# Recurrent-memory attention and feed-forward kernel: merged transposes, token sums earlier, flushed fill work, outputs in row order, and a regrouped preparation of the feed-forward part

## The chip, the cores and the metric

The kernel runs on one core of one Trainium2 chip. The metric is device microseconds of one execution, the median of several. The core has five engines that run their own instruction streams and wait for each other by semaphores: TensorE (PE; its weight loads are listed as PEld), VectorE (DVE), ScalarE (ACT), GpSimd (POOL) and SyncE (SP, which here only issues DMAs). PE adds up in PSUM buffers, from which ACT and DVE copy ("evacuate") results to SBUF.

## The reference

B = 1, S = 2048 tokens, D = 640, 32 heads of 128, 8 memory rows, segments of 32 tokens, F = 1728; bfloat16 in and out.

```python
mem = mem0
for s in range(S // 32):                       # 64 segments, one after another
    h = concat([mem, layernorm(x)[s*32:(s+1)*32]])      # 8 + 32 rows
    q, k, v = h @ Wq, h @ Wk, h @ Wv                    # per head
    p = softmax(where(mask, q k^T / sqrt(128), -1e9))   # the 8 memory rows see all 40 keys,
                                                        # a token the keys up to its own
    o = (p v) @ Wo
    mem = o[:8]                                # feeds the next segment
    outs.append(o[8:])
h = x + concat(outs)
out = h + relu(layernorm(h) @ w1 + b1)**2 @ w2 + b2
```

## The kernel before, in words

The 64 segments form NB = 16 blocks of four steps (sp = 0 to 3); each step is one segment, and the memory rows that leave a step enter the next one through mem_to_hT (L283), so the steps are a serial chain. A step works on 32 rows in its main path: 8 memory rows and the first HD = 24 tokens. The last TL = 8 tokens of the four segments of a block are taken together as a "tail" of 32 rows, since nothing in the chain needs them at once. The tail's q, k and v passes of block b + 1 are cut into units (tail_pass_fill, L241: ten units of four matmuls for each of q, k and v, and for q and k two "late" units that transpose the row), the tail's output projection of block b - 1 into eight units (wo_tail_fill, L268). These units wait in the list `fill`, and run_fill(n) (L236) runs n of them at places in a step where the chain would leave PE without work: three (F1) after the memory softmax's sums, four (F2) before the output projection, two after it and one behind mem_to_hT.

main_step (L341) goes through a step in this order: two q passes of 20 matmuls each (half, L206 for the matmuls; evacuation in L199 on ACT or L201 on DVE); the token values of the step before (token_values, L307); the first k pass, a transpose of the first half of q (turn, L219: four 128x128 transposes, then one 512-wide evacuation), the second k pass, the second half of q, the first half of k; twelve matmuls of the first v pass, the second half of k, eight more; twelve of the second v pass; scores (L385, L389); the exponentials on ACT (L392 for the memory columns, L398 for tokens, L400 for the tail); two masks on Pool (L402, L403); the memory softmax's sums pz (L408), its reciprocal rz and diagonal rd on DVE, the values po (L425), the spread reciprocal pb (L429), rs on ACT (L432), oT on DVE (L436); then the output projection wo_pass (L226), 128 matmuls with the function sums (L444) in its middle: four one-row sums pzk (L448, L450), their reciprocal rk on DVE (L453), a spread copy rb on Pool (L454). Behind the projection two transposes pr (L461) turn rb over, and DVE writes the normalized token weights pnk and pnl (L463, L464), which token_values uses in the next step.

The order on PE, ACT, DVE and Pool is the order of the code down to order.close() (L513); after it a scheduler sets it. PSUM has two "mm" buffers (all passes, output projections, and fill units from their first to their last), two "pt" buffers (transposes and small sums) and four for values. Each step's o goes to DRAM by one DMA (o_main, L304), each block's tail by one (o_tail, L279).

The start loads wq, wk, wv in chunks of 128 rows on SP; their fifth chunk is packed into the partitions by four DMAs of 32 rows each on ACT's queue (L171), and wo is split between SP and ACT.

The feed-forward part (FFN) goes through four tiles t of NT = 512 tokens. prep(t) (L538) loads for each of its four blocks of 128 rows x and eight pieces of o_main and o_tail, adds them (L549), takes the layernorm's statistics (L118, L121) on DVE, its root by fourteen small Pool operations (L122 to L129), applies it (L139), transposes on PE (L554), evacuates on ACT (L556), and adds b2 on Pool (L558). Then come 14 groups of five matmuls (L567) with relu on ACT (L570) and the square on DVE (L571), prep(t + 1), and 8 groups of 14 matmuls (L582) with the last add (L584) and the output's DMA. The FFN's weights take the place of wq in the last step.

## Time and profile before

| what | value |
|---|---|
| median of 5 runs | 1388.39 us (1386.1 to 1396.4) |
| the profiled execution's own time | 1388.16 us |
| its span | 1386.5 us |
| PE / DVE / ACT / POOL busy | 88% / 36% / 34% / 18% of the span |
| first main q pass of block 1, of block 15, start of the last step | 128.83, 1118.80, 1167.30 us |
| first FFN matmul | 1220.83 us |

The span runs from the first to the last instruction in the trace; 1.66 us of the profiled execution lie around it. A row of the timeline has the start, the duration, engine, line, operation, `out<-in` by the program's tile names (`ps` and `pw` PSUM of a pass and of an output projection, `pt` of transposes, `hT` and `hTt` the transposed inputs of main path and tail), how many instructions were put together, and in brackets the idle time ahead and what ended it. Matmuls overlap in the pipeline, so a group's cost is best read from its start to the next group's start.

### The profile page before, as it was taken

To read this page: it belongs to the slowest core of one execution; us is meant where nothing else is said; L and a number is where in the kernel's file an instruction comes from. 1 tells how busy PE (TensorE), PEld (TensorE's weight loads), DVE (VectorE), ACT (ScalarE), POOL (GpSimd) and SP (SyncE) were. 2 spreads that over 40 slices of the span, in tenths; PEclk is the share of its full clock that TensorE was granted. 3 is DMA by queue.
4 is the path that set the end of the run, shared out by engine and by line. 5 is a ranking of instruction groups with operands and counts; after the bars stand their busy time and mean duration, and the time that the engine had idled before them with its cause. 6 is when DMAs were issued, how large, how long until landed. Compare 5 with 4: busy or idle time off the path is not lost.

```text
span 1386.5 us, 69365 instructions
## 1 busy us (share of the span) xinstructions
PE 1215.0 (88%) x32248; PEld 704.4 (51%) x32248; DVE 503.5 (36%) x1400; ACT 465.4 (34%) x1001; POOL 256.4 (18%) x813
## 2 busy tenths in 40 slices
PE   0699999899999999989998999999999998378879
PEld 0255555555555555555555555555555555334444
DVE  1033434343334343433333334343434334234332
ACT  0233333333333333333333343333333333033212
POOL 4011111111111111111111112121212111334340
PEclk9899999999999999999999999999999999679999
DMA  9900000000000000000000000000000002402200
GB/s 230 378 27 6 12 6 12 6 13 6 12 6 12 6 12 6 12 6 12 6 12 4 12 6 12 6 12 6 8 6 8 6 7 80 121 19 58 55 23 20
DMA packets 37762, 43.92 MB, mean 32 GB/s; under 512 B 22816, under 2 KB 34880, under 8 KB 35552
## 3 DMA queue, kind: packets, MB, share of 16 engines
q1 hardware_dynamic: 34400, 33.46, 8.1%
q10 hardware_dynamic: 2656, 5.77, 1.5%
q8 instruction: 252, 4.13, 1.2%
q0 software_dynamic: 416, 0.26, 0.1%
q14 instruction: 38, 0.31, 0.1%
HBM read 33.44 MB, written 5.94 MB: 28 GB/s over the span
## 4 chain that ended last, share of the span: by engine, by line
PE 75%; DVE 6%; DMA 5%; ACT 5%; issue 4%; POOL 3%; SPq 1%; ACTq 0%; POOLq 0%; DVEq 0%
PE ps L206 39%; PE pw L226 11%; PE pt L219 6%; PE psy L582 4%; PE ps L226 3%; ACT row L199 2%; DMA wq<-in_A_Wq_dram 2%; PE psf L567 2%; PE po L425 2%; DVE row L201 2%; PE pss L389 1%; DMA wk<-in_A_Wk_dram 1%; PE po L312 1%; PE pss L385 1%; PE po L318 1%
## 5 line engine op out<-in xcount | busy, mean ns | idle before, releaser
L206 PEld LDWEIGHTS <-hT 128*32 128x32 bf16 x7680 | 179.4, 96 | 203.2 <-issue 45.3
L199 ACT CAST row<-ps 128x512 bf16<-128x512 f32 x192 | 112.7, 587 | 329.7 <-PE ps L206 313.8
L206 PE MATMUL ps<-wv,hT 128*32 128x512 bf16 x2560 | 177.8, 383 | 15.5 <-DVE vr L201 12.0
L226 PE MATMUL pw<-wo,oT 128*32 128x160 bf16 x8320 | 174.0, 235 | 17.2 <-issue 9.4
L201 DVE CAST row<-ps 128x512 bf16<-128x512 f32 x128 | 88.5, 691 | 232.4 <-PE ps L206 232.4
L206 PE MATMUL ps<-wk,hT 128*32 128x512 bf16 x2560 | 161.6, 381 | 8.5 <-ACT row L199 5.3
L226 PEld LDWEIGHTS <-oT 128*32 128x32 bf16 x8320 | 148.6, 98 | 37.5 <-issue 17.3
L206 PE MATMUL ps<-wq,hT 128*32 128x512 bf16 x2560 | 153.0, 381 | 14.2 <-ACT row L199 11.0
L219 PEld LDWEIGHTS <-row 128*128 128x128 bf16 x1280 | 76.0, 98 | 105.7 <-issue 98.6
L402 POOL TENSOR_TENSOR pk_s<-pk_s,mask_m 128x192 bf16<-128x192 bf16 x64 | 45.7, 714 | 439.6 <-ACT pk_s L398 439.5
L219 PE MATMUL pt<-ident,row 128*128 128x128 bf16 x1280 | 113.6, 222 | 14.2 <-DVE rz L416 9.8
L324 POOL COPY oTt<-oT 128x256 bf16<-128x256 bf16 x64 | 25.6, 400 | 315.8 <-DVE oT L201 310.5
L201 DVE CAST vr<-ps 128x512 bf16<-128x512 f32 x64 | 44.3, 692 | 109.2 <-PE ps L206 109.2
L199 ACT COPY kT<-pt 128x512 bf16<-128x512 bf16 x128 | 75.3, 589 | 17.6 <-PE pt L219 17.5
L582 PE MATMUL psy<-fw,fk 128*128 128x320 bf16 x448 | 73.1, 313 | 0.0
L199 ACT CAST oT<-po 128x256 bf16<-128x256 f32 x128 | 41.5, 375 | 93.2 <-PE po L318 93.2
L567 PE MATMUL psf<-fk,fw 128*128 128x512 bf16 (+1 forms) x280 | 63.8, 387 | 5.8 <-ACT fv L570 3.5
L206 PEld LDWEIGHTS <-hTt 128*32 128x32 bf16 x1920 | 40.3, 97 | 55.8 <-issue 24.4
L199 ACT COPY qT<-pt 128x512 bf16<-128x512 bf16 x64 | 37.4, 585 | 88.5 <-PE pt L219 88.5
L454 POOL CAST rb<-rk 128x256 bf16<-128x256 f32 x64 | 26.4, 412 | 193.8 <-DVE rk L453 193.8
L436 DVE TENSOR_TENSOR oT<-po,rs 128x128 bf16<-128x128 f32 x128 | 31.3, 286 | 74.2 <-ACT rs L432 74.2
L206 PE MATMUL ps<-wq,hTt 128*32 128x512 bf16 x640 | 48.2, 397 | 10.9 <-DMA wq<-in_A_Wq_dram 6.7
(108 smaller groups left out, 1480.7 us busy)
## 6 DMA issues: line engine op xcount, KB each, us to landing
wq<-in_A_Wq_dram SPq DMA_DIRECT2D x4, 1024.0 KB
wk<-in_A_Wk_dram SPq DMA_DIRECT2D x4, 1024.0 KB
wv<-in_A_Wv_dram SPq DMA_DIRECT2D x4, 1024.0 KB
o_main<-o SPq DMA_DIRECT2D x65, 40.0 KB
xt<-in_A_x_dram SPq DMA_DIRECT2D x16, 160.0 KB
wo<-in_A_Wo_dram ACTq DMA_DIRECT2D x2, 1280.0 KB
wo<-in_A_Wo_dram SPq DMA_DIRECT2D x2, 1280.0 KB
fv<-in_A_x_dram SPq DMA_DIRECT2D x16, 160.0 KB
```

Of the source, the lines that this page charges most:

```text
L199: nc.scalar.copy(out=out_, in_=in_)
L201: nc.vector.tensor_copy(out=out_, in_=in_)
L206: nc.tensor.matmul(ps[32 * g:32 * g + 32, :], lhsT=lhs(c), rhs=w[:, c, g * EG + n * 512:g * EG + (n + 1) * 512], start=(c == 0), stop=(c = ...
L219: nc.tensor.transpose(out=pt[:, k * 128:(k + 1) * 128], in_=row[:, i * 128:(i + 1) * 128], identity=ident[:])
L226: nc.tensor.matmul(ps[32 * g:32 * g + 32, 0:DG], lhsT=lhs(h), rhs=wo[:, h, g * DG:(g + 1) * DG], start=(h == 0), stop=(h == H - 1))
L324: nc.gpsimd.tensor_copy(out=oTt[:, :, sp * TL:(sp + 1) * TL], in_=oT[:, :, SEG:NQ])
L402: nc.gpsimd.tensor_tensor(out=pkh, in0=pkh, in1=mask_m[:], op=ALU.mult)
L425: nc.tensor.matmul(po[:, i * SEG:(i + 1) * SEG], lhsT=v[:, i * E:(i + 1) * E], rhs=pbd[:, a, i].rearrange("p g q -> p (g q)"), start=(a == ...
L436: nc.vector.tensor_tensor(out=oT[:, k * 16:(k + 1) * 16, 0:M].rearrange("p (g i) q -> p g i q", g=2), in0=pov[:, gs], in1=rs[:].rearrange( ...
L454: nc.gpsimd.tensor_copy(out=rb[:], in_=rk[:].unsqueeze(2).to_broadcast([128, 2 * G, SEG]))
L567: nc.tensor.matmul(ps[0:fs, :], lhsT=w1[:, c, fc * 128:fc * 128 + fs], rhs=hnT[:, c, :], start=(c == 0), stop=(c == DC - 1))
L582: nc.tensor.matmul(ps[:, 0:320], lhsT=f1T[0:fs, fc, k * 128:(k + 1) * 128], rhs=w2[0:fs, fc, cs], start=(fc == 0), stop=(fc == FC - 1))
```

## The change

- turn() transposes all eight chunks of a row in one visit and evacuates 1024 columns at once: q's on ACT, k's on DVE. Both turns stand behind the first v pass, which is now in one piece.
- The token sums come from a matmul with a block matrix of ones (onesblk), which gives them already spread: two matmuls right behind pb. The reciprocal is taken on 256 columns; rb, the two pr matmuls and sums() are gone, the output projection is in one piece, and pnk and pnl stand behind mem_to_hT.
- run_fill counts microseconds written into the code (0.22 for a pass unit, 0.29 for an output unit, 0.6 for a late turn) instead of units: 0.8, 0.9 and 0.4 at three places, and everything that is left at the step's end. The late turns come one step later.
- o is written in row order to one DRAM tensor a_rows: four DMAs a step of 24x160 and sixteen a block of 8x160 instead of one each. The FFN loads one 128x640 piece of it a block.
- The fifth weight chunks go DRAM to DRAM (w4s) by twelve DMAs on ACT's queue, and come back as one 128-partition load each on SP. All of wo is loaded on SP.
- prep is split: prep_loads, prep_rows (adds, statistics, one root for four blocks, applies, b2 adds) and prep_turn (transposes). prep_rows(0) stands ahead of the last token_values; in the FFN loop loads and rows for t + 1 stand ahead of the fc loop and the transposes behind it. The FFN's weights and the first rows are loaded in the last step; the output leaves in halves.

On ACT, a step before, from the evacuation of k's row: one evacuation for q's second half, two for k, the exponentials (`p`, `pk_s`, `p_lz`), and then evacuations of fill units among the rest.

```order
L199 CAST row<-ps 128x512
L199 COPY qT<-pt 128x16x32
L199 COPY kT<-pt 128x512 x2
L392 ACTIVATE p<-pss 128x8x2x8
L199 CAST vr<-ps 128x512
L398 ACTIVATE pk_s<-pss 128x256
L400 ACTIVATE p_lz<-pss 128x8x8
L199 CAST row<-ps 128x512
L199 COPY kTt<-pt 128x512
L432 COPY rs<-pb 128x256
```

The same stretch of ACT's stream now:

```order
L208 CAST row<-ps 128x512
L208 COPY qT<-pt 128x32x32
L439 ACTIVATE p<-pss 128x8x2x8
L208 CAST vr<-ps 128x512
L448 ACTIVATE pk_s<-pss 128x256
L450 ACTIVATE p_lt<-pss 128x64
L482 COPY rs<-pb 128x256
```

q's evacuation has become one for the whole row, k's have gone to DVE, and the evacuations of the fill units come after rs.

On PE, before, the token sums in the middle of the output projection (`pw` is the projection, LDWEIGHTS loads the operand that stays in the array; the brackets name the engines whose semaphores are waited for).

```order
L226 MATMUL pw<-wo,oT 32x160
L448 LDWEIGHTS pk_s [waits Pool_49]
L448 MATMUL pzk<-ones_76,pk_s 128x4 [waits Activation_49]
L450 LDWEIGHTS p_lz [waits Pool_49]
L450 MATMUL pzk<-ones_76,p_lz 128x4
L448 LDWEIGHTS pk_s
L448 MATMUL pzk<-ones_76,pk_s 128x4
L450 LDWEIGHTS p_lz
L450 MATMUL pzk<-ones_76,p_lz 128x4
L226 LDWEIGHTS oT [waits DVE_49]
L226 MATMUL pw<-wo,oT 32x160
```

On PE now, behind the spread reciprocal pb of the memory rows:

```order
L475 MATMUL po<-pbd,vt 128x32
L479 LDWEIGHTS ones_109
L479 MATMUL pb<-rd,ones_109 128x256 [waits DVE_49]
L484 LDWEIGHTS onesblk [waits PE_49,Activation_49]
L484 MATMUL pzk<-pk_s,onesblk 128x256 [waits Pool_49]
L485 LDWEIGHTS onesblk
L485 MATMUL pzk<-p_lt,onesblk 128x8x8 [waits Pool_49]
L215 LDWEIGHTS hTt
L215 MATMUL ps<-wv,hTt 32x512
```

The sums and their two waits for Pool's masks stand ahead of the second fill and of the whole output projection instead of in its middle.

On DVE, before, the end of attention (`pnk` and `pnl` are the last step's token weights, `oT` the last token values, `o` the last output) and the first block of prep(0):

```order
L463 TENSOR_TENSOR pnk<-pk_s,pr 128x256
L464 TENSOR_TENSOR pnl<-p_lz,pr 128x64
L201 CAST oT<-po_36946 128x8x32
L201 CAST oT<-po_36948 128x8x32
L231 CAST o<-pw 128x160
L549 TENSOR_TENSOR fv<-fv 128x640
L118 BN_STATS lnst<-fv 128x6 x2
L121 BN_AGGR lnmv<-lnst 128x2
L139 TENSOR_SCALAR fv<-fv,lnmv,lnrs 128x640
```

The same place on DVE now (from the last of four adds with statistics that stand behind pnl):

```order
L383 TENSOR_TENSOR fv<-fv 128x640
L115 BN_STATS lnst<-fv 128x6 x2
L386 BN_AGGR fmv<-lnst 128x2
L132 TENSOR_SCALAR fv<-fv,fmv,lnrs 128x640 x4
L210 CAST oT<-po_36725 128x8x32
L210 CAST oT<-po_36727 128x8x32
L383 TENSOR_TENSOR fv<-fv 128x640
L115 BN_STATS lnst<-fv 128x6 x2
```

The four adds, statistics and applies of prep_rows(0) have come ahead of the copies of the last token values, and the adds of t = 1 follow at once.

The core of the diff:

```diff
-        def turn(row, j, dst, eng):
+        def turn(row, dst, eng):
             pt = psum_t.tile([128, 1024], BF16, tag="pt", name="pt")
-            for k in range(4):
-                i = j * 4 + k
+            for i in range(HG):
...
-            evac(eng, dst, pt[:, 0:512].rearrange("p (i g r) -> p i g r", i=4, g=G))
+            evac(eng, dst, pt[:].rearrange("p (i g r) -> p i g r", i=HG, g=G))
...
-        def run_fill(n, eng="act"):
-            while n > 0 and fill:
-                fill.pop(0)(eng)
-                n -= 1
+        def run_fill(us, eng="act"):
+            while us > 0.1 and fill:
+                f, t = fill.pop(0)
+                f(eng)
+                us -= t
...
             half(wk, lhs, 0, kr, "act")
-            turn(qr, 0, qT[:, 0:4, :, 0:SEG], "dve")
             half(wk, lhs, 1, kr, "dve")
-            turn(qr, 1, qT[:, 4:8, :, 0:SEG], "act")
-            turn(kr, 0, kT[:, 0:4], "act")
...
+            half(wv, lhs, 0, vr, "dve")
+            turn(qr, qT[:, :, :, 0:SEG], "act")
+            turn(kr, kT[:], "dve")
...
+            pzk = psum_t.tile([128, 512], F32, tag="pt", name="pzk")
+            nc.tensor.matmul(pzk[:, 0:NK], lhsT=onesblk[:], rhs=pk_s[:], start=True, stop=False, skip_group_check=True)
+            nc.tensor.matmul(pzk[:, 0:NK].rearrange("p (i q) -> p i q", q=SEG)[:, :, HD:SEG], lhsT=onesblk[:],
+                             rhs=p_lt[:], start=False, stop=True, skip_group_check=True)
...
-            run_fill(F2)
...
-            o = wo_pass(b * 4 + sp, sums)
...
+            rk = s1.tile([128, NK], F32, tag="rs", name="rk")
+            nc.vector.reciprocal(out=rk[:], in_=pzk[:, 0:NK])
+            run_fill(0.9)
...
+            o = wo_pass(b * 4 + sp)
+            run_fill(0.4)
...
-            run_fill(1)
+            nc.vector.tensor_tensor(out=pnk[:], in0=pk_s[:], in1=rk[:], op=ALU.mult)
...
+            run_fill(100)
...
+            for g in range(G):
+                nc.scalar.dma_start(out=w4s[wi, g * DR:(g + 1) * DR, :], in_=w2d[g * DG + 128:(g + 1) * DG, :])
...
+            nc.sync.dma_start(out=w[:, 4, :], in_=w4s[wi])
...
-            nc.sync.dma_start(out=o_main[s], in_=o[:])
+            if s > 0:
+                for g in range(G):
+                    nc.sync.dma_start(out=a_rows[(s - 1) * SEG:(s - 1) * SEG + HD, g * DG:(g + 1) * DG],
+                                      in_=o[32 * g + M:32 * g + SEG, :])
...
+        def prep_rows(t):
+            mv = s2.tile([128, NK4, nc.vector.BN_AGGR_DIM], F32, tag="fmv", name="fmv")
+            for k in range(NK4):
+                st = s2.tile([128, 2, nc.vector.BN_STATS_DIM], F32, tag="lnst", name="lnst")
+                nc.vector.tensor_tensor(out=ots[k], in0=ots[k], in1=xs[k], op=ALU.add)
+                for j in range(2):
+                    ln_stats(st, j, ots[k])
+                nc.vector.bn_aggr(out=mv[:, k, :], in_=st[:])
+            rstd = ln_root(s2, mv, NK4)
+            for k in range(NK4):
+                ln_apply(hns[k], ots[k], mv, rstd, k)
+            for k in range(NK4):
+                nc.gpsimd.tensor_tensor(out=hbs[t % 2 * NK4 + k], in0=ots[k], in1=b2b[0], op=ALU.add)
...
+        prep_rows(0)
         token_values(*pend.pop())
         wo_pass(S // SEG)
...
-        prep(0)
+        prep_turn(0)
         for t in range(S // NT):
             hnT, f1T = hnTs[t % 2], f1Ts[t % 2]
+            if t + 1 < S // NT:
+                prep_loads(t + 1)
+                prep_rows(t + 1)
...
             if t + 1 < S // NT:
-                prep(t + 1)
+                prep_turn(t + 1)
```

237 lines of the change are left out of this document (108 added, 129 removed).

## The prediction

> **What bounds the kernel now.** I read the page first, for the busy shares, then the windows, which cut the span into its stages.
>
> ```profile
> PE 1215.0 (88%) x32248; PEld 704.4 (51%) x32248; DVE 503.5 (36%) x1400; ACT 465.4 (34%) x1001; POOL 256.4 (18%) x813
> ```
>
> The columns of the windows are: from and to, length, busy time and instructions of PE, PEld, DVE, ACT and POOL, the granted clock, the DMA share and GB/s.
>
> ```profile
> 0.00:40.00 40.00, 7.65 (x70) 3.35 (x74) 5.96 (x28) 3.57 (x5) 15.52 (x57) 1.00 0.97 238
> 40.00:75.47 35.47, 23.55 (x444) 11.70 (x436) 5.40 (x15) 7.92 (x16) 1.75 (x5) 0.81 0.92 346
> 75.47:128.83 53.36, 49.64 (x1404) 28.28 (x1406) 19.93 (x56) 20.33 (x45) 7.75 (x23) 1.00 0.03 6
> 128.83:1118.80 989.97, 924.67 (x27402) 543.46 (x27398) 374.77 (x1061) 363.07 (x812) 155.62 (x468) 1.00 0.03 9
> ...
> 1186.32:1220.83 34.51, 9.29 (x277) 7.93 (x278) 8.80 (x23) 3.03 (x5) 16.71 (x61) 0.60 0.29 70
> 1220.83:1386.50 165.67, 140.66 (x788) 73.17 (x787) 63.71 (x148) 46.08 (x68) 50.34 (x180) 0.96 0.12 33
> ```
>
> So there are four stages with four limits. Up to 75.47 us the weights' DMAs limit (DMA share 0.97 and 0.92). Blocks 1 to 14 take 989.97/14 = 70.71 us each, and PE is busy for 924.67/14 = 66.05 of it: there PE's own work is the limit, with 4.7 us of gaps. Between attention and FFN, PE works 9.29 us of 34.51. The FFN takes 165.67 us, of which PE works 140.66.
>
> Where blocks 1 to 14 lose time stands in PE's waits (sum in us, times, longest):
>
> ```profile
> PE ps L206 <- ACT row L199: 15.2, 28, 0.7
> PE ps L206 <- DVE vr L201: 11.2, 14, 0.8
> PE pt L219 <- DVE rz L416: 9.1, 14, 0.7
> PE pw L226 <- issue: 7.4, 12, 1.1
> PE ps L206 <- DVE row L201: 6.3, 28, 0.2
> ```
>
> Fourteen or 28 times means once or twice a block, so one of the four steps is slow. The timeline of PE in block 7 shows it (start, duration, number of matmuls, wait ahead):
>
> ```profile
> 585.34 2.34 PE L206 MATMUL ps<-wq,hT 128*32 128x512 bf16 x40
> 602.10 1.26 PE L206 MATMUL ps<-wq,hT 128*32 128x512 bf16 x20
> 604.10 1.26 PE L206 MATMUL ps<-wq,hT 128*32 128x512 bf16 x20 [0.73 <-ACT row L199]
> 608.10 1.26 PE L206 MATMUL ps<-wk,hT 128*32 128x512 bf16 x20 [0.35 <-ACT row L199]
> 612.66 0.83 PE L206 MATMUL ps<-wv,hT 128*32 128x512 bf16 x12 [0.80 <-DVE vr L201]
> 622.23 2.33 PE L206 MATMUL ps<-wq,hT 128*32 128x512 bf16 x40
> ```
>
> Step 2 (585.34 to 602.10) takes 16.76 us, step 3 takes 20.13. At 585.34 both halves of q follow each other without a break, at 602.10 the second half waits until the first has been evacuated. The reason is in the code: step 2 queues 12 fill units (two late transposes, ten of the k pass) and runs ten, so a half-summed k tail keeps one of the two "mm" buffers through step 3's five passes, and each must wait for the other buffer to be emptied.
>
> **The blocks, part by part.** *Waits that go.* The change flushes the fill list at each step's end, so no half-summed tail is left. ACT row, DVE vr and DVE row are 32.7 us, the rz wait 9.1 (a tail transpose in the first fill that waits for a "pt" buffer; now a pass unit comes first): 41.8/14 = 3.0 us a block. Idle time counts less than is lost: the second q half starts 2.00 us after the first instead of the 1.2 that 20 matmuls take, 0.80 lost against 0.73 recorded, and smaller gaps are not listed. At most it is the 4.7 of all gaps, less the issue waits (7.4/14 = 0.5), which stay: I take 4.2, the upper end, since the listed rows are only the longest.
>
> *Work on PE.* Turning q and k costs three visits to the transposes now, and one later:
>
> ```profile
> 590.91 0.62 PE L219 MATMUL pt<-ident,row 128*128 128x128 bf16 x8
> 591.46 0.83 PE L206 MATMUL ps<-wv,hT 128*32 128x512 bf16 x12
> 592.23 0.40 PE L219 MATMUL pt<-ident,row 128*128 128x128 bf16 x4
> 592.55 1.26 PE L206 MATMUL ps<-wv,hT 128*32 128x512 bf16 x20
> ```
>
> By starts, 8 transposes hold PE 0.55 us and 4 hold it 0.32, so one is 0.057 and a visit 0.09. Before it is 0.32 + 0.55 + 0.32 = 1.19; 16 at once are 16 x 0.057 + 0.09 = 1.00: -0.19 a step. The sums of the token softmax move too:
>
> ```profile
> 582.56 0.18 PE L448 MATMUL pzk<-ones,pk_s 128*128 128x4 bf16 x1
> ...
> 582.74 1.29 PE L226 MATMUL pw<-wo,oT 128*32 128x160 bf16 x64
> 583.96 0.28 PE L461 MATMUL pr<-ident,rb 128*128 128x128 bf16 x2
> 584.18 0.62 PE L206 MATMUL ps<-wq,hTt 128*32 128x512 bf16 x8
> ```
>
> The four pzk matmuls (0.18) and the two pr (0.22) leave; two matmuls of 256 and 64 columns come, behind pb in the same tile shape: the pr pair moves 256 columns too, so 0.2 (0.1 to 0.3). That is -0.2. With one visit instead of two for each tail transpose (0.09 each, two a block), PE loses about 0.39 x 4 + 0.2 = 1.8 us of work a block.
>
> *New waits.* The pair behind pb now needs both Pool masks early; before, half of the output projection lay between. Pool's and PE's rows in block 7's step 1 (the step that starts at 585.34):
>
> ```profile
> 595.75 0.71 POOL L402 TENSOR_TENSOR pk_s<-pk_s,mask_m 128x192 bf16<-128x192 bf16 x1 [6.12 <-ACT pk_s L398]
> 596.43 0.30 POOL L403 TENSOR_TENSOR p_lz<-p_lz,mask_t 128x64 bf16<-128x64 bf16 x1
> 594.83 0.17 PE L408 MATMUL pz<-ones4t,p 128*64 128x4 bf16 x1
> ```
>
> Pool ends at 596.73. From pz at 594.83, four units of 0.24 us (a fifth of the 1.2), po and pb (about 0.7) bring PE to 596.5: it waits 0.2 us a step (0 to 0.4), and everything behind it on PE, fill and output projection, waits along. The second new wait is the 1024-wide evacuation of qT on ACT, which the scores need:
>
> ```profile
> L199 ACT COPY qT<-pt 128x512 bf16<-128x512 bf16 x64 | 37.4, 585 | 88.5 <-PE pt L219 88.5
> L556 ACT COPY fk<-pt 128x640 bf16<-128x640 bf16 x16 | 11.0, 688 | 99.2 <-PE pt L554 99.2
> ```
>
> 128 columns more cost 103 ns, so 1024 cost 585 + 4 x 103 = 1.0 us. Turn k (0.5) and twelve v matmuls (0.75) hide it with 0.2 to spare, about the hand-over at its two ends: 0 to 0.3, I take 0.1. If that cover went, it would cost the whole 1.0. Beside them, in the two steps where nothing is left to flush behind mem_to_hT, the next q pass waits for the copy of hT, which one unit (0.24) covers now: 0 to 0.24 each, I take 0.1. Together 0.3 x 4 + 0.2 = 1.4.
>
> By the Trainium skill ("Perfetto Trace Analysis", Optimizing Scalar/DVE Operations), grouping helps if ACT or DVE is saturated, and where they are not but cause bubbles on other engines, smaller instructions may let work complete sooner. Here ACT is 34% busy and DVE 36%, so the rule speaks against the merged evacuations; it is rival A. Before's trace agrees as far as PE did wait for such copies (15.2 us for ACT row), but those were waits for a buffer, not for a copy's length.
>
> Sum for a block: -4.2 - 1.8 + 1.4 = -4.6, from -1.8 (waits -3.0, work -1.4, new waits 2.6 with 0.6 a step) to -6.5 (-4.7 - 1.8, nothing new): **14 x 4.6 = -64 us**. Steps 1 to 3 of block 0 have the same carry: -3.5. Block 15 has no tails to fill: -1.
>
> **Start.** Twelve weight pieces no longer load into 32 partitions each but go DRAM to DRAM and are read back as three full rows; wo queues behind them on SP.
>
> ```profile
> 61.60 3.18 PE L206 MATMUL ps<-wv,hTt 128*32 128x512 bf16 x28 [2.64 <-DMA wv<-in_A_Wv_dram]
> 71.45 1.29 PE L226 MATMUL pw<-wo,oT 128*32 128x160 bf16 x64 [0.79 <-DVE oT L436]
> ```
>
> wv's last piece holds PE until 61.60, and the output projection is 9.9 us behind. 15.7 MB of wq, wk and wv without wo between (2.6 MB of it came on ACT's queue) would land earlier, but 3.1 MB are moved twice; at the windows' 346 GB/s they are 9 us, about what wo's first half took (2.6 MB, 7.6 us). I take -4, between -8 and +5: no row shows a DRAM to DRAM copy.
>
> **Junction.** The rows are of DVE's applies, of PE's first FFN matmul, of the DMA issues (the last number is us from issue to landing) and of PE's start of the last step.
>
> ```profile
> 1206.41 0.45 DVE L139 TENSOR_SCALAR fv<-fv,lnmv,lnrs 128x640 bf16<-128x640 bf16 x1 [4.18 <-POOL lnrs L129]
> ...
> 1212.62 0.45 DVE L139 TENSOR_SCALAR fv<-fv,lnmv,lnrs 128x640 bf16<-128x640 bf16 x1 [4.18 <-POOL lnrs L129]
> 1220.83 11.63 PE L567 MATMUL psf<-fk,fw 128*128 128x512 bf16 x45 [0.78 <-ACT fk L556]
> mask_m<-mask_m POOLq DMA_DIRECT2D x3, 12.0 KB, 6.5
> 1167.30 2.34 PE L206 MATMUL ps<-wq,hT 128*32 128x512 bf16 x40 [0.30 <-DVE hT L289]
> ```
>
> From the last step's start to the first FFN matmul are 1220.83 - 1167.30 = 53.5 us. Now four blocks go one after another, 6.21 us each, of which 4.18 is waiting for a root on Pool and 6.21 - 4.18 - 0.45 = 1.6 the add and the statistics. Later one root serves four. But prep_rows(0) stands ahead of the last token values on DVE. Counted from the step's start: its loads can start when wv is read for the last time (about +11, as 612.66 stands to 602.10), land 6.5 later at +18 (the nearest landing), four adds with statistics end at +24, root and four applies at +30. Only then come the oT copies, the output projection and the tail, for which I take the 9.3 us that PE works in the window from 1186 at clock 0.60: +40. Before FFN t = 0 PE also has, in its order, the transposes of t = 1's first block; DVE does t = 1's four adds (6.4) behind the oT copies, to +38, and the root on Pool queues behind four hb adds: 4 to 6 more, apply and transposes, +46. That is **-7** (0 to -14).
>
> **FFN.**
>
> ```profile
> 1263.18 12.05 PE L567 MATMUL psf<-fk,fw 128*128 128x512 bf16 x55
> ...
> 1285.28 0.45 PE L554 MATMUL pt<-ident,fv 128*128 128x128 bf16 x5 [3.43 <-DVE fv L139]
> ...
> 1307.35 13.11 PE L567 MATMUL psf<-fk,fw 128*128 128x512 bf16 x60 [0.78 <-ACT fk L556]
> ...
> 1350.94 15.39 PE L567 MATMUL psf<-fk,fw 128*128 128x512 bf16 x70 [0.78 <-ACT fk L556]
> ```
>
> From 1220.83 on the loops take 42.35, 44.17, 43.59 and, the last without a preparation in it, 35.56 us. With preparation ahead of the fc loop the first three come near 35.6 + 1.2 for 20 transposes = 37: 130.1 - 111 = -19; since the adds sit between the relu squares on DVE, -17 (-10 to -20).
>
> **Sum.** -64 - 3.5 - 1 - 4 - 7 - 17 = -96.5. The profiled run took 1388.16 us for a span of 1386.5; the median is 1388.39, 0.2 more. 1388.4 - 96.5 = 1291.9, so **1292 us**.
>
> **Rivals.** *A, the new waits eat the steady gain.* If the two waits cost 0.65 a step more than I put them (half of qT's 1.0 uncovered, pzk at 0.4), 4 x 0.65 = 2.6 of the 4.6 is eaten: 14 x 2.6 = +36, 1328 us. For it: Pool and ACT are in the chain of each step. Against: in the rows above the cover is as long as the evacuation. 0.12.
> *B, slower.* Outputs go to DRAM as 4 small writes a step and 16 a block, 33 DMAs a block with x instead of 6, and the program hands them eight semaphores in turn, each DMA waiting for the one eight before. SP then lasts 33/8 landings a block. It decides from 66/4.1 = 16 us a landing; at 20 us a block takes 82 us, 14 x (82 - 70.7) = +158, less 24 for junction and FFN: 1522.
>
> ```profile
> SPq L304 <- DVE o L231: 866.7, 64, 19.7
> 1209.63 0.34 SPq L545 DMA_DIRECT2D fv<-o_main  x1
> ```
>
> Against: SP waits 866.7 us for o, an issue takes 0.34, and the small landing above is 6.5. 0.03. The Trainium skill ("DMA: Bandwidth & Descriptors", Bandwidth) calls transfers under 64 KB descriptor-dominated, which speaks against pieces of 2.5 and 7.5 KB; by it the loss stays on an idle queue. No row of before shows how long such a write takes to land.
> *C, the junction gains nothing* or loses a few us, its chain being serial: 1299 to 1304. 0.15.
> *D, staging through DRAM is slow*, wv lands 10 us later: 1306. 0.05.
> My forecast has the remaining 0.65.
>
> **Numbers.** Cases C and D lie inside the range. Above it are most of A and B, 0.12; below it the case that all gaps go (-6 a block, FFN -20), 0.08 under 1268. Range **1268 to 1314**, with 0.2 left out. A measurement of this kernel can tell about 0.5%, 7 us, from no change: only B lies above 1395, and a stronger A near 1388. Faster 0.94, same 0.02, slower 0.04.
>
> **What would show it.** In the changed profile: blocks of 66.1 us; no PE wait for "ACT row" 28 times; step 3 as long as step 2; pzk's wait for Pool at 0.2 a step, qT's at 0.1; first FFN matmul 46 us after the last step's start; loops of 37 us; first output projection near 67 us. I am wrong if a step waits for qT or Pool over 0.6 us, or the blocks stay above 68.

## The result, and the profile after

The changed kernel takes **1263.78 us** (median of 8 runs, 1258.95 to 1266.42), 0.9086 of the kernel before (95% interval 0.907 to 0.9103; before had a median of 1390.5 us in 15 runs). It is faster, as forecast, but by 127 us where 96 were forecast; the time lies 4 us under the range's lower end of 1268. The profiled execution, the longest of the eight, has a span of 1264.7 us, so the sum below is 5 us short of the medians' change. By stages, from the first main q pass of each step and the first FFN matmul of each tile:

| stage | before | after | change | forecast |
|---|---|---|---|---|
| to the start of step 1 | 75.5 | 69.3 | -6.2 | -4 |
| steps 1 to 3 of block 0 | 53.4 | 49.2 | -4.2 | -3.5 |
| blocks 1 to 14, each | 70.71 | 64.85 | -5.86 | -4.6 |
| the same, together | 990.0 | 907.9 | -82.1 | -64 |
| block 15 to its last step | 48.5 | 47.4 | -1.1 | -1 |
| last step to first FFN matmul | 53.5 | 51.1 | -2.4 | -7 |
| FFN | 165.7 | 139.9 | -25.8 | -17 |
| sum | 1386.5 | 1264.7 | -121.8 | -96.5 |

The page's busy line and the windows of the changed kernel (columns as before):

```profile
PE 1164.3 (92%) x31992; PEld 695.7 (55%) x31992; DVE 617.4 (49%) x1404; ACT 424.0 (34%) x841; POOL 201.0 (16%) x581
```

```profile
118.41:1026.26 907.85, 883.05 (x27176) 534.84 (x27175) 472.49 (x1062) 327.64 (x672) 135.66 (x415) 1.00 0.04 9
...
1088.88:1124.79 35.91, 12.69 (x428) 11.38 (x428) 21.40 (x46) 3.32 (x6) 17.54 (x37) 0.64 0.44 126
1124.79:1264.70 139.91, 135.32 (x785) 71.61 (x783) 53.80 (x131) 45.61 (x68) 17.68 (x36) 0.98 0.12 34
```

In blocks 1 to 14 PE is now busy for 883.05 of 907.85 us: 63.1 us of work a block (66.05 before) and 1.8 us of gaps (4.7 before). The FFN's gaps fell from 25 us to 4.6. PE's waits in the blocks, and step 3 of block 7, which took 20.13 us and now takes 571.34 - 555.40 = 15.94:

```profile
PE pw L234 <- issue: 9.7, 11, 1.6
PE ps L215 <- DVE hT L302: 4.3, 14, 0.3
PE ps L234 <- issue: 4.1, 3, 1.6
```

```profile
555.40 2.34 PE L215 MATMUL ps<-wq,hT 128*32 128x512 bf16 x40
...
558.25 2.34 PE L215 MATMUL ps<-wk,hT 128*32 128x512 bf16 x40
560.42 1.25 PE L215 MATMUL ps<-wv,hT 128*32 128x512 bf16 x20
561.61 1.07 PE L227 MATMUL pt<-ident,row 128*128 128x128 bf16 x16
562.61 0.83 PE L215 MATMUL ps<-wv,hT 128*32 128x512 bf16 x12
563.39 0.37 PE L432 MATMUL pss<-qT,kTt 128*32 128x16 bf16 x32
...
564.51 0.19 PE L458 MATMUL pz<-ones,p 128*64 128x4 bf16 x1
...
567.72 2.40 PE L234 MATMUL pw<-wo,oT 128*32 128x160 bf16 x128
569.93 0.62 PE L215 MATMUL ps<-wv,hTt 128*32 128x512 bf16 x8
```

In the list of waits, none for "ACT row", "DVE vr", "DVE row" or rz is left, and none for qT or for Pool's masks has come. But short waits don't appear in that list; they have to be read from the rows. These are ACT, Pool and PE in step 2 of block 7:

```profile
546.35 1.01 ACT L208 COPY qT<-pt 128x1024 bf16<-128x1024 bf16 x1 [1.96 <-PE pt L227]
```

```profile
550.18 0.30 POOL L453 TENSOR_TENSOR p_lt<-p_lt,mask_t 128x64 bf16<-128x64 bf16 x1
```

```profile
547.41 0.37 PE L432 MATMUL pss<-qT,kTt 128*32 128x16 bf16 x32
...
550.54 0.19 PE L485 MATMUL pzk<-p_lt,onesblk 128*128 128x64 bf16 x1
```

qT is written at 547.36, and the scores start at 547.41; in all 56 steps of blocks 1 to 14 they start 0.05 us behind the end of qT's copy. The twelve v matmuls ahead of them last 0.78 us up to the scores (562.61 to 563.39 above); before they lasted 0.64 (612.66 to 613.30). So PE does wait for qT, 0.13 us in every step, near the 0.1 that the prediction took. The merged copy takes 1.01 us, as worked out. The tail's mask ends at 550.48 and its sum runs at 550.54: the second matmul of the pair stands 0.16 us behind the first, and 0.12 in the run with the sums alone, so this wait is about 0.04 us a step.

A third short wait stands where the output projection starts:

```profile
551.15 0.58 ACT L208 CAST row<-ps 128x512 bf16<-128x512 f32 x1 [0.24 <-PE ps L215]
...
551.79 2.40 PE L234 MATMUL pw<-wo,oT 128*32 128x160 bf16 x128
```

The second fill stops in the middle of a sum here too. That unit holds one "mm" buffer, and the projection needs the other, which ACT has emptied at 551.73. In 42 of the 56 steps the projection starts 0.05 us behind such an evacuation, 0.42 to 0.46 us after the last fill matmul where it is 0.21 otherwise: about 0.7 us a block (before it came in one step of each block and cost 0.43 there). The held buffer is the same mechanism as theory H below, still at work in the changed kernel.

### The profile page after: what moved, and what is told of

Read it like the earlier page. It is cut to its first block, busy times and chain, and to the rows that moved or that the text cites. A ratio compares the mean times of both kernels' runs of the same rounds, so it can differ in the third digit from the quotient of the medians.

```text
span 1264.7 us, 68777 instructions
## 1 busy us (share of the span) xinstructions
PE 1164.3 (92%) x31992; PEld 695.7 (55%) x31992; DVE 617.4 (49%) x1404; ACT 424.0 (34%) x841; POOL 201.0 (16%) x581
## 4 chain that ended last, share of the span: by engine, by line
PE 85%; DMA 6%; DVE 3%; issue 2%; SPq 2%; POOL 1%; ACT 1%; ACTq 0%; POOLq 0%; DVEq 0%
PE ps L215 42%; PE pw L234 12%; PE pt L227 6%; PE psy L590 4%; PE psf L575 4%; PE ps L234 3%; PE po L475 2%; PE pss L432 2%; PE po L322 1%; DMA fv<-a_rows 1%; PE pss L436 1%; PE po L328 1%; DMA wk<-in_A_Wk_dram 1%; DMA wo<-in_A_Wo_dram 1%; PE pz L458 1%
## 5 line engine op out<-in xcount | busy, mean ns | idle before, releaser
L215 PEld LDWEIGHTS <-hT 128*32 128x32 bf16 x7680 | 185.3, 96 | 176.7 <-DVE hT L302 8.5
L234 PE MATMUL pw<-wo,oT 128*32 128x160 bf16 x8320 | 164.5, 237 | 20.1 <-issue 11.5
L234 PEld LDWEIGHTS <-oT 128*32 128x32 bf16 x8320 | 153.2, 99 | 42.4 <-issue 32.4
L215 PE MATMUL ps<-wk,hT 128*32 128x512 bf16 x2560 | 150.1, 381 | 0.0
L493 DVE RECIPROCAL rk<-pzk 128x256 f32<-128x256 f32 x64 | 112.5, 1758 | 7.0 <-DVE oT L490 0.5
L208 ACT COPY qT<-pt 128x1024 bf16<-128x1024 bf16 x64 | 64.8, 1012 | 137.2 <-PE pt L227 137.2
L227 PE MATMUL pt<-ident,row 128*128 128x128 bf16 x1280 | 89.0, 221 | 1.2 <-issue 0.7
L208 ACT CAST oT<-po 128x256 bf16<-128x256 f32 x128 | 41.4, 375 | 84.3 <-PE po L328 84.3
L590 PE MATMUL psy<-fw,fk 128*128 128x320 bf16 x448 | 68.7, 300 | 0.3 <-DVE fk L579 0.3
L578 ACT ACTIVATE fw<-psf,b1f 128x512 bf16<-128x512 f32 (+1 forms) x56 | 38.4, 687 | 74.4 <-PE psf L575 71.4
L210 DVE CAST vr<-ps 128x512 bf16<-128x512 f32 x64 | 44.2, 691 | 35.1 <-PE ps L215 35.1
L462 DVE TENSOR_TENSOR pbd<-p,ones 128x256 bf16<-128x256 bf16 x64 | 27.2, 425 | 69.3 <-ACT p L439 69.3
```

Of the source, the lines that this page charges most:

```text
L208: nc.scalar.copy(out=out_, in_=in_)
L210: nc.vector.tensor_copy(out=out_, in_=in_)
L215: nc.tensor.matmul(ps[32 * g:32 * g + 32, :], lhsT=lhs(c), rhs=w[:, c, g * EG + n * 512:g * EG + (n + 1) * 512], start=(c == 0), stop=(c = ...
L227: nc.tensor.transpose(out=pt[:, i * 128:(i + 1) * 128], in_=row[:, i * 128:(i + 1) * 128], identity=ident[:])
L234: nc.tensor.matmul(ps[32 * g:32 * g + 32, 0:DG], lhsT=lhs(h), rhs=wo[:, h, g * DG:(g + 1) * DG], start=(h == 0), stop=(h == H - 1))
L462: nc.vector.tensor_tensor(out=pbd[:, a], in0=p[:, a].unsqueeze(2).to_broadcast([128, HG, G, M]), in1=on[a].unsqueeze(1).unsqueeze(3).to_br ...
```

## The experiments

Each run has the time of the kernel before on the same chip beside it (1391 to 1394 us); "us less" is against that. Blocks, junction (last step's start to the first FFN matmul) and loops are read from the profile of each run.

| run | median | blocks | junction | FFN loops 1, 2, 3 |
|---|---|---|---|---|
| before | 1388.4 | 70.71 | 53.5 | 42.4, 44.2, 43.6 |
| changed | 1263.8 | 64.85 | 51.1 | 35.9, 34.8, 33.5 |
| flush only | 1348.4 | 67.91 | | |
| turns only | 1375.4 | 69.68 | | |
| sums only | 1378.2 | 69.87 | | |
| place only | 1391.6 | 70.90 | 55.2 | 40.4, 43.6, 43.1 |
| carry half / whole | 1324.8 / 1288.5 | 68.82 / 66.36 | | |
| four roots | 1291.7 | 64.89 | 68.2 | 40.3, 37.2, 33.5 |
| eight loads | 1277.0 | 64.82 | 57.5 | 38.5, 36.3, 36.5 |
| roots and loads | 1285.3 | 64.99 | 59.4 | 41.7, 38.0, 34.5 |
| old pieces | 1303.0 | 64.99 | 61.3 | 42.2, 43.6, 42.3 |
| one load, before | 1362.4 | 70.95 | 45.3 | 41.4, 33.9, 33.5 |
| whole output | 1266.4 | 65.00 | 50.6 | 35.4, 34.5, 33.5 |
| no staging | 1270.8 | 65.04 | 49.8 | 35.1, 34.9, 33.5 |
| rows behind | 1268.0 | 64.89 | 41.4 | 38.1, 40.9, 33.5 |
| loads on Pool | 1266.6 | 64.99 | 41.4 | 38.7, 40.6, 33.5 |
| rows in loop | 1288.3 | 64.85 | 41.8 | 47.2, 44.4, 44.4 |
| turns in psy | 1254.2 | 64.55 | 40.9 | 36.4, 34.2, 34.2 |

### Parts of the change in the kernel before

Flush only:

```diff
                 mem_to_hT(o, hT4s[b + 1], 0)
-            run_fill(1)
+            run_fill(100)
```

> The kernel before with one edit: at each step's end all that is left in the fill list runs, instead of one unit. Theory H (a half-summed tail unit holds one of the two mm buffers through step 3): step 3 falls from 20.0 to about 16.7 us, of which 0.5 goes to step 2 with two moved units, so 2.8 us a block, 15 blocks, 42 us less: 1348 us, and PE's waits for 'ACT row', 'DVE vr' and 'DVE row' in blocks 1 to 14 (32.7 us) are gone. Rival R1 (step 3 stalls because ACT and DVE have more to evacuate there than elsewhere): the waits stay, under 10 us less, 1380 or above.

Measured: 1348.42 us, ratio 0.9671 (0.9654 to 0.9689), 44 us less. PE's waits in blocks 1 to 14:

```profile
PE pt L219 <- DVE rz L416: 18.3, 28, 0.7
PE pw L226 <- issue: 8.8, 12, 1.3
PE pw L226 <- ACT row L199: 3.6, 14, 0.3
```

The passes' three waits for a buffer are gone, so theory H holds to a few us; the projection's wait for "ACT row" is as before. The rz wait comes 28 times now, not 14: the late turns stand first in the fill of step 3 as well, and nothing hides it there any more. So the flush is worth 3.4 us a block, and 0.65 of it goes to that wait.

Turns only, with the old four-transpose turn kept for the tails:

```diff
-            turn(qr, 0, qT[:, 0:4, :, 0:SEG], "dve")
             half(wk, lhs, 1, kr, "dve")
-            turn(qr, 1, qT[:, 4:8, :, 0:SEG], "act")
-            turn(kr, 0, kT[:, 0:4], "act")
...
+            half(wv, lhs, 0, vr, "dve")
+            turn8(qr, qT[:, :, :, 0:SEG], "act")
+            turn8(kr, kT[:], "dve")
```

> The kernel before with merged turns of q and k in the main path only (eight transposes, one 1024-wide evacuation, both behind the first v pass). Theory V (each visit to another tile shape costs PE about 0.1 us; the merged copies are covered): 0.22 us a step, 64 steps, 14 us less, 1376 us, no wait of PE for qT or kT. Rival A (the merged copy, 1.0 us on ACT, uncovers a wait of the scores): 0.1 to 0.5 us a step more, so 1383 to 1408 us, with a wait of PE for qT 64 times.

Measured: 1375.4 us, 0.9867 (0.9849 to 0.9886), 17 us less. PE's list has one wait for qT in 14 blocks (0.2 us). By the rows the shorter one is there in every step: the twelve v matmuls last 0.78 us up to the scores, 0.13 more than before. So rival A's wait comes, at the low end of its 0.1 to 0.5 us, but the edit gains more than it costs.

Sums only (pzk by the block of ones behind pb, reciprocal of 256 columns, no rb, no pr, the projection in one piece):

> The kernel before with the token sums by the block of ones behind pb, the 256-wide reciprocal, no rb and no pr, and the output projection in one piece. Theory V: the two visits inside and behind the projection cost more than the 0.40 us of their own starts, because the projection pays again when it resumes; 0.35 to 0.55 us a step less, so 22 to 35 us, about 1362 us. Rival V0 (only the visits' own 0.40 counts and the new pair takes 0.27): 0.13 a step, 8 us, 1382. Rival A (pzk waits for Pool's masks 0.2 to 0.4 a step): no gain, 1385 to 1395, with that wait 64 times in PE's list.

Measured: 1378.22 us, 0.9886 (0.9867 to 0.9905), 14.5 us less or 0.23 a step: between V and V0, and no wait for Pool's masks in PE's list. The cut of the projection costs something beyond the 0.40 of its own starts, but less than V had it; in the changed kernel's rows the projection is 0.62 us shorter (2.83 to 2.21, shown further down).

Flush, turns and sums together take 2.8 + 1.03 + 0.84 = 4.67 of the 5.86 us a block. The next pair shows where the rest is.

### A buffer held, or not

Both runs are the changed kernel with the late turn of q first in step 2's fill and no flush there; they differ in one number.

```diff
-                    fill += prev_late
+                    if sp == 2:
+                        fill += prev_late + us
...
-            run_fill(100)
+            if sp != 2:
+                run_fill(100)
...
-            run_fill(0.4)
+            run_fill(0.4 if sp != 2 else 0)     # carry whole only
```

> The changed kernel, in which step 2 runs its late turn of q first and isn't flushed, so that three of the ten k units are left for step 3, in the middle of a sum: a half-summed tail holds an mm buffer through step 3. Theory H: step 3 stalls again, 2.8 us a block, and the turn in the first fill of step 2 waits for rz, 0.65 us, so 15 x 3.4 = 52 us more, 1316 us. Rival R1 (the amount of evacuation decides, held buffer or not): as the run that carries five whole units, within 5 us of it.

> As the run before, but five k units are left, a whole sum: the buffer has been evacuated and is free in step 3, though more work is carried over. Theory H: no stalls in step 3's passes; only the rz wait of 0.65 us, 15 x 0.65 = 10 us more, 1274 us. Rival R1: step 3 has even more to evacuate, so it is at least as slow as with three units carried, about 1316 us.

Measured: 1324.81 us with three units carried in the middle of a sum, 1288.48 us with five units carried at the end of one (0.9504, 0.946 to 0.9549, and 0.9245, 0.9206 to 0.9283). PE's waits in blocks 1 to 14 of the first and of the second:

```profile
PE ps L215 <- ACT row L208: 19.8, 28, 0.7
PE ps L215 <- DVE row L210: 14.1, 28, 0.8
PE pt L227 <- DVE rz L466: 9.2, 14, 0.7
```

```profile
PE pt L227 <- DVE rz L466: 9.2, 14, 0.7
PE ps L215 <- DVE hT L302: 8.6, 28, 0.3
PE pm L298 <- DVE o L239: 6.1, 14, 0.4
```

The run with more work carried is 36 us faster, so it is the held buffer, not the amount of evacuation; H holds and R1 falls. The second run also has the rz wait back for the place of a single turn (9.2/14 = 0.66 us a block), and 24.7 us more than the changed kernel where 10 were forecast, since the copy of o is uncovered once a block, by the edit's own run_fill(0), and that of hT once more than in the changed kernel: 0.44 + 0.31 + 0.66 = 1.4 of its 1.5 us a block. The late turn that comes last in the fill is thus the missing part: before 0.65 a block, in flush only 1.3, in the changed kernel none. 4.67 + 1.3 = 5.97, against 5.86 measured.

### The FFN

Place only moves loads, adds, roots and applies for t + 1 ahead of the fc loop, in the kernel before. It also gives the normalized rows four rooms instead of two, as they need there:

```diff
+            if t + 1 < S // NT:
+                prep_rows(t + 1)
             for fc in range(FC):
...
-                prep(t + 1)
+                prep_turn(t + 1)
```

> The kernel before, in which only the place of the FFN's preparation changes: loads, adds, statistics, a root for each block and the applies for t + 1 stand ahead of the fc loop, its transposes behind it; the 36 loads for each t and the four roots stay. Theory P (the place alone frees PE): the first three loops fall from 42.4, 44.2 and 43.6 us to about 34 to 35, 24 to 27 us in all, 1363 to 1366 us. Rival L (the number of loads and roots decides; 36 loads at 0.34 us take 12 us of SP for each t): the loops stay above 40 us, less than 10 us gained.

Measured: 1391.62 us, 0.9989 (0.9972 to 1.0005), no change: theory P, on which the prediction's FFN term rests, falls. The place in the code doesn't decide it, since behind order.close() the scheduler writes the order: PE's instruction stream is the same as before, row for row. In the changed kernel the streams of all five engines stay the same, row for row, if prep_loads and prep_rows are put back behind the fc loop.

Four roots and eight loads undo one thing each in the changed kernel, roots and loads both:

```diff
-            rstd = ln_root(s2, mv, NK4)
+                rstd = ln_root(s2, mv, 1)                    # four roots: in the loop over blocks
...
-                nc.sync.dma_start(out=ots[k], in_=a_rows[b * 128:(b + 1) * 128, :])
+                for j in range(8):                           # eight loads
+                    nc.sync.dma_start(out=ots[k][j * 16:(j + 1) * 16, :],
+                                      in_=a_rows[b * 128 + j * 16:b * 128 + (j + 1) * 16, :])
```

> The changed kernel with one root for each block of 128 rows, as before, instead of one for four. Theory G (the chain of four roots of 4.2 us, with DVE waiting in line for each, is what the FFN loops lost): the first three loops rise from 35.9, 34.8 and 33.5 us to 40 or more, 18 to 24 us; the preparation ahead of the FFN gets three roots longer, up to 12 us; 1282 to 1300 us. Rival L (the number of loads decides): the loops stay at 36 or below, and only the junction grows: up to 1276.

> The changed kernel with eight loads of 16 rows for each block instead of one load of 128 rows, so 36 loads for each t as before. Theory G: loads are issued early and the loops stay at 36 or below; at the junction up to 8 us (28 more issues of 0.3 us ahead of the adds); 1264 to 1272. Rival L (loads decide): the loops rise to 40 or more, 18 to 24 us on top: 1282 to 1296.

> The changed kernel with both a root for each block and eight loads for each block. Alone the roots cost the three loops 6.8 us and the loads 7.1. Theory J (the two share one chain: a late load delays every root behind it, so that together they undo the FFN's gain): first three loops at 40 to 44 us, 16 to 24 more than in the changed kernel, and the junction at 68 or more: 1297 to 1312 us. Rival K (the rest of the gain has another cause, four rooms for the normalized rows or the output in halves): loops near 14 us more in all, 39 us each or less, 1295 or below.

Measured: 1291.68, 1276.97 and 1285.26 us (0.927, 0.923 to 0.931; 0.9167, 0.9129 to 0.9205; 0.9217, 0.9195 to 0.9239). The roots cost the loops 6.8 us and the junction 17; the loads 7.1 and 6.4; both together cost the loops 10.1, so J falls, and neither G nor L holds alone. 130.1 - 114.3 = 16 us stayed open. Two runs look for it: the changed kernel with four roots and also o_main and o_tail as before, and the kernel before with a_rows.

> The changed kernel with four roots and with the old form of the outputs: one write a step and one a block to o_main and o_tail, and 36 loads for each t, eight of them a block in strided pieces. Theory Y (the form of the pieces, four runs of 320 bytes in each row, makes the loads late): the first three loops come to 125 to 131 us together, as in the kernel before (130.1), against 114.3 with eight whole-row pieces and four roots; 1295 to 1305 us. Rival Z (what is left of the FFN's gain comes from preparing t = 1 in the junction, by the order that follows from prep_rows standing ahead of the end of attention): 111 to 117 us, 1283 to 1291. In both, blocks 1 to 14 stay at 64.9 us, since the small writes cost nothing.

> The kernel before with the outputs of attention written in row order by the small DMAs (33 a block) and one load for each block in the FFN; four roots, attention and all else as before. Theory for the small writes: SP has room, blocks 1 to 14 stay at 70.7 us. Rival B: the blocks grow. For the FFN, if the loads alone carry most of its gain: first three loops at 36 or below, 20 us or more less, junction some us less: 1362 to 1370. If they carry their share of 7 us: 1380 to 1386.

> The changed kernel with one output DMA for each block of 128 rows instead of two halves. If the halves carry the rest of the FFN's gain: first three loops 3 to 5 us longer each, 1273 to 1280. If they carry nothing: 1263 to 1266, loops as in the changed kernel.

Measured: old pieces 1302.95 us (0.9367, 0.9348 to 0.9387) with loops of 128.1 us; one load in the kernel before 1362.35 (0.9758, 0.9726 to 0.9791), 32 us less; whole output 1266.38 (0.9072, 0.9047 to 0.9098), no difference from the changed kernel. PE at the second loop's end and in the third with one load in the kernel before:

```profile
1273.15 0.73 PE L555 MATMUL pt<-ident,fv 128*128 128x128 bf16 x10
1273.72 0.84 PE L583 MATMUL psy<-fw,fk 128*128 128x320 bf16 x5
1274.57 0.44 PE L555 MATMUL pt<-ident,fv 128*128 128x128 bf16 x5
...
1291.36 15.40 PE L568 MATMUL psf<-fk,fw 128*128 128x512 bf16 x68
```

The transposes stand between the output matmuls without a wait, where before one had 3.43 us in brackets; this with four roots and the old code of prep. So the loads of whole rows, one a block instead of eight strided ones, carry most of the FFN's gain: loops -21.3 of the -25.9 us, junction -8.2. The strided form alone costs 128.1 - 114.3 = 13.8 us of loops (Y; old pieces against roots and loads, which differ in the small writes too). One root for four blocks adds its share beside fast loads as well: four roots cost the changed kernel's loops 6.8 us, and loop 1 takes 41.4 us with one load in the kernel before against 35.9 changed. Why roots and loads together take 6 us less than the roots alone stays open; it is the junction that differs (59.4 against 68.2). The same two runs settle rival B of the prediction: with 33 small DMAs a block the old kernel's blocks take 70.95 us against 70.71, and without them the changed kernel's take 64.99 against 64.85. The small writes cost nothing that shows. By the Trainium skill ("DMA: Bandwidth & Descriptors", Bandwidth) pieces under 64 KB are descriptor-dominated; for these writes no run shows a cost, while for the loads, which DVE waits for, number and form of the pieces together are worth 21 us. That the writes are free because nothing waits for them soon is argued, not tried; SP still waits 647.3 us for o in the changed kernel.

### Start and junction

No staging puts the 32-row pieces back on ACT's queue and leaves wo on SP:

> The changed kernel without the staging in DRAM: the fifth weight chunks load as 32-row pieces into the partitions on ACT's queue again, while all of wo stays on SP behind wq, wk and wv. Theory S (the 32-row pieces slow all loads down, 238 against 374 GB/s in the first 40 us): the first main q pass goes back from 33.7 to about 38 us and the second step's start from 69.3 to about 75: 1269 us. Rival O (it is the order of wo that counts): both stay within 1.5 us: 1264.

Measured: 1270.75 us (0.9114, 0.9095 to 0.9133). The first main q pass is at 37.6 instead of 33.7, step 1 at 73.6 instead of 69.3, and the first 40 us move 252 GB/s instead of 374. S holds: 4.4 of the 6.2 us come from the staging. This is one profile of each; step 1 starts at 71.9 to 76.3 us in the kernels with the old start and at 68.6 to 69.8 in those with the new one, so the staging's gain is clear of the spread, and a share of wo's new place is not. DRAM to DRAM copies aren't slow here.

Rows behind moves one line:

```diff
-        prep_rows(0)
         token_values(*pend.pop())
+        prep_rows(0)
         wo_pass(S // SEG)
```

> The changed kernel with prep_rows(0) behind the last token_values instead of ahead of it; all else the same. Theory C (the junction lost because DVE keeps the last oT copies behind four adds, a root on Pool and four applies, and PE waits 11.4 us for it): the copies come at about 20 us after the last step's start instead of 38, the first FFN matmul at about 38 to 42 instead of 51: 1251 to 1255 us. Rival C2 (the loads and the instruction fetches of PE decide): less than 4 us, 1260 or above.

Measured: 1267.99 us (0.909, 0.9069 to 0.9111), no gain. The junction falls by 9.7 us, as C has it, but loops 1 and 2 give 8.4 of it back. PE, then DVE in loop 2:

```profile
1166.60 12.10 PE L575 MATMUL psf<-fk,fw 128*128 128x512 bf16 x45 [5.11 <-ACT fw L578]
```

```profile
1162.61 0.49 DVE L383 TENSOR_TENSOR fv<-fv 128x640 bf16<-128x640 bf16 x1 [2.52 <-DMA fv<-a_rows]
...
1167.69 0.49 DVE L383 TENSOR_TENSOR fv<-fv 128x640 bf16<-128x640 bf16 x1 [1.59 <-DMA fv<-a_rows]
```

These adds belong to a later tile; squares stand behind them in DVE's line, relu waits for the squares' rooms, PE for relu. If the queue made these loads late, another queue would help:

```diff
+            q = nc.gpsimd if t else nc.sync
...
-                nc.sync.dma_start(out=ots[k], in_=a_rows[b * 128:(b + 1) * 128, :])
+                q.dma_start(out=ots[k], in_=a_rows[b * 128:(b + 1) * 128, :])
```

> The changed kernel with prep_rows(0) behind the last token_values (as in the run rows behind) and the FFN's loads for t of 1 and more issued on Pool's queue instead of SP's. Theory Q (rows behind lost its 9.7 us again because its a_rows loads stand on SP's queue behind outputs that wait for DVE, and DVE's adds, squares and outputs queue behind those loads): the loops return to 33.5 to 36 us with the junction at about 41, 1254 to 1257 us, faster than the changed kernel by over 0.5%. Rival Q2 (the loops stretch for the order on DVE, not for late loads): loops as before, 1265 to 1270.

Measured: 1266.64 us (0.9074, 0.905 to 0.9099). Q falls: DVE waits 3.90 and 3.65 us for a_rows all the same.

```profile
1151.02 0.49 DVE L384 TENSOR_TENSOR fv<-fv 128x640 bf16<-128x640 bf16 x1 [3.90 <-DMA fv<-a_rows]
...
1156.96 0.49 DVE L384 TENSOR_TENSOR fv<-fv 128x640 bf16<-128x640 bf16 x1 [3.65 <-DMA fv<-a_rows]
```

Then the order itself was changed: written by hand through the FFN, with t + 1's adds behind the squares of groups 4 to 7.

> The changed kernel with prep_rows(0) behind the last token_values and the FFN's order written by hand too: t + 1's adds with statistics behind the squares of groups 4 to 7, root and b2 adds behind them on Pool, the applies behind groups 12 and 13, transposes behind the fc loop. Theory W (in the run rows behind, adds of two tiles ahead wait on DVE for loads whose rooms are free only after later b2 adds, with squares and outputs in line behind): junction 41, loops 33.5 to 34.5 each, 1251 to 1256 us, faster than the changed kernel by 0.6 to 1%. Rival W2 (the end of attention loses it elsewhere, or the handwritten order adds waits of its own): 1262 or above.

Measured: 1288.25 us (0.9267, 0.9245 to 0.9289): W2, by a wait that this order made itself:

```profile
PE pt L559 <- DVE fv L132: 26.3, 13, 4.4
```

All four transposes stood ahead of the output matmuls and waited for applies that wait for the root. In the last run they stand behind the first three blocks' output matmuls, and the four applies behind the last square:

```diff
-            if t + 1 < S // NT:
-                prep_turn(t + 1)
...
+                if t + 1 < S // NT:
+                    prep_turn(t + 1, ((0,), (1, 2), (3,), ())[k])
```

> As rows in loop, but the four applies stand behind the last square and t + 1's transposes behind the first, second and third block's output matmuls, so that neither DVE nor PE has anything in line behind the root. Theory W (what rows in loop lost are PE's 13 waits for the applies, which its own order made): loops 33.5 to 35 each, junction 41 to 42, 1251 to 1256 us, faster than the changed kernel by 0.6 to 1%. Rival W2 (the clock or the b2 adds on Pool, which slow the applies, cost as much): 1262 or above.

Measured: **1254.16 us** (0.902, 0.9005 to 0.9034), faster than both kernels; its interval lies under the changed kernel's (0.907 to 0.9103). PE at the end of loop 1:

```profile
1132.41 0.45 PE L559 MATMUL pt<-ident,fv 128*128 128x128 bf16 x5
1132.69 4.28 PE L612 MATMUL psy<-fw,fk 128*128 128x320 bf16 x28
1136.91 0.73 PE L559 MATMUL pt<-ident,fv 128*128 128x128 bf16 x10
```

No transpose waits, and the loops are 36.4, 34.2 and 34.2 us with the junction at 40.9. The changed kernel's loops come to 104.2 us together, these to 104.8: the gain is the junction's 10.2 us, which the loops no longer give back. So W holds for the order as a whole, though loop 1 lies 1.4 us above its 35. What makes a_rows late two tiles ahead can be read from the trace of rows behind, on Pool and SP:

```profile
1153.33 1.39 POOL L391 TENSOR_TENSOR fv<-fv,fk 128x640 f32<-128x640 bf16 x1 [2.03 <-DVE fv L592]
```

```profile
1154.75 0.33 SPq L377 DMA_DIRECT2D fv<-a_rows  x1
```

The b2 add on Pool waits for the output's last add, which frees its room, and the next a_rows load is issued 0.03 us after the b2 add has ended (again at 1160.17 and 1160.19). No run moves the b2 adds by themselves.

## Why the prediction was right and wrong

**The blocks: mechanism right, the work on PE mis-sized.** Waits that go were put at 4.2 us a block. Flush (2.8, with 0.65 more of the rz wait against it) and the late turn's place (1.3) make 4.1. Work that goes (1.8) and new waits (1.4) were to come to -0.4 together; they came to 5.86 - 4.1 = -1.8, and that is the 18 us by which the block term was too small. The step that failed is "PE loses about 0.39 x 4 + 0.2 = 1.8 us of work a block": it priced each visit to another tile shape by its own starts. PE before, in step 2 of block 7, and the scores of step 3:

```profile
588.19 1.26 PE L206 MATMUL ps<-wk,hT 128*32 128x512 bf16 x20
...
594.78 0.19 PE L408 MATMUL pz<-ones,p 128*64 128x4 bf16 x1
...
598.11 1.28 PE L226 MATMUL pw<-wo,oT 128*32 128x160 bf16 x64
...
600.94 0.62 PE L206 MATMUL ps<-wk,hTt 128*32 128x512 bf16 x8
...
613.30 0.40 PE L385 MATMUL pss<-qT,kTt 128*32 128x16 bf16 x32
```

From the first k pass to the memory softmax's sums pz PE took 6.59 us (588.19 to 594.78) and now takes 6.26 (558.25 to 564.51), though the 0.13 of waiting for qT is in it: 0.46 of work has gone where 0.19 was counted. The projection with what stood in and behind it took 2.83 us (598.11 to 600.94) and takes 2.21 (567.72 to 569.93); the new pair ahead of it takes 0.28, 0.04 of it waiting, so 0.38 has gone where 0.2 was counted. That is 0.84 us a step, 3.4 a block: the passes and the projection run faster uncut, beyond what the visits' own starts show. The new waits were nearly of the forecast size: 0.5 us a block for qT, 0.2 for the masks (0.8 was forecast), 0.3 for hT, and 0.3 net at the projection, which the prediction did not have, 1.3 in all. These parts add to the measured 5.86 only to within some 0.4; turns only and sums only, 1.03 + 0.84 = 1.9, measure work and waits net.

Rival A's waits came, but small. The rule that it leaned on ("Perfetto Trace Analysis", Optimizing Scalar/DVE Operations, of the Trainium skill: smaller instructions where an unsaturated engine causes bubbles) comes true by the 0.13 us that the scores wait for the 1.01 us copy; the merged turns save more on PE, so that turns only is 17 us faster. Two slips in the prediction change no sum: the step that starts at 585.34 is step 2 of block 7, and the new pair (128*128) is not in the tile shape of pb (64*128).

**The FFN, wrong in its reason and too small.** The term rested on "with preparation ahead of the fc loop", and place only shows that as worth nothing. The gain comes from loads of whole rows, an edit that the prediction priced at nothing. Its size was too small for a second reason: the last loop was taken as one without preparation, 35.56 us, but that stretch has the kernel's end in it.

```profile
1366.26 16.96 PE L582 MATMUL psy<-fw,fk 128*128 128x320 bf16 x112
```

The last matmul of before ends at 1383.22 of 1386.5, so the loop itself is 32.28 us, and 33.5 with the transposes, which is what the third loop takes now: 35.56 - 32.28 = 3.3 us for each of three loops, 10 us that the sum lacked. The first two loops, at 35.9 and 34.8, still lie above 33.5.

**The junction, too hopeful.** -7 was forecast, -2.4 came, from one pair of profiles; the kernels with before's end of attention take 53.5 to 55.2 us here, those with the changed kernel's 49.8 to 51.1, so it is some 4 us and still short of 7. The order of events was right: DVE's copies of oT are the last thing, behind adds, root and applies.

```profile
1105.97 5.90 DVE L132 TENSOR_SCALAR fv<-fv,fmv,lnrs 128x640 bf16<-128x640 bf16 x4 [3.99 <-POOL lnrs L128]
1111.79 0.74 DVE L210 CAST oT<-po 128x256 bf16<-128x256 f32 x2
```

```profile
1088.88 2.99 PE L234 MATMUL pw<-wo,oT 128*32 128x160 bf16 x83 [1.88 <-issue]
...
1095.93 0.30 PE L328 MATMUL po<-pnl,vt 32*128 32x8 bf16 x19 [2.81 <-issue]
...
1107.63 0.71 PE L560 MATMUL pt<-ident,fv 128*128 128x128 bf16 x5 [11.41 <-DVE fv L132]
...
1124.79 17.72 PE L575 MATMUL psf<-fk,fw 128*128 128x512 bf16 x70
```

The step that failed is "root and four applies at +30": the first add ran at 1095.75, 22 us after the step's start and not 18, and the four applies took 5.90 us instead of 4 x 0.45, so the copies came at +38 instead of +30. From there to the first FFN matmul it took 13.0 us where 16 were counted, so +51 instead of +46. Rows behind shows that 9.7 us were to be had there.

**Start, and what was small.** -6.2 against -4, within its bounds; the first output projection came at 62.71, not near 67, and then PE waited 2.63 us for wo. Block 0 and block 15 as forecast. Rival B (small writes) and D (staging) fell; C came half true inside the range. The forecast's sign, the held buffer and the two largest terms were right; the range was too narrow below: the case under its end had -6 a block with an FFN of -20, and the blocks came at -5.86 beside an FFN of -25.8.

## What to carry to other kernels

A fill unit that stops in the middle of a sum holds a PSUM buffer, and the passes behind it pay for it, not the fill: end sums before the next stage, and look for waits that come a fixed number of times a block. The place where fill work stops before an output projection is such a stage boundary too. Price a visit to another tile shape by the stretch around it, from the start of the pass before to the start of the one behind, and not by its own starts alone. When a new dependence is as long as what covers it in the rows, expect a wait of about a tenth of a us and read it from the starts, since a list of waits may not show it. When a reference stretch is taken as undisturbed, cut off what else lies in it. Behind a scheduler, moving code may move nothing: compare the orders first, and when a stage's wait is won, look where DVE's or PE's line hands it back.
